# Attention and two MoE layers on one core: the first head pair's q and k transposed on TensorE instead of by DMA

## The chip, the cores and the metric

The kernel runs on one NeuronCore of a Trainium2 chip. Five engines work side by side, each through its own queue of instructions in order: TensorE (PE in the profile, its weight loads PEld), VectorE (DVE), ScalarE (ACT), GpSimd (POOL) and SyncE (SP), which here issues nearly all DMAs. The metric is the device time of one execution in microseconds, the median of several runs; lower is better.

## What is computed

Attention with a top-32 mask per row over 4 x 8 heads of 576 rows and 64 columns, a feed-forward layer with softplus on the 2304 tokens, and a layer of 8 experts of which each token uses one:

```
scores = scale * q @ k^T                    # 4 batches, 8 heads, 576 x 576
kth    = 32nd largest of each row
scores = where(scores >= kth, scores, -1e9)
attn   = softmax(scores);  x = attn @ v     # heads side by side: 2304 x 512
g      = softplus(x @ w_in) @ w_out         # 512 -> 2048 -> 512
e      = argmax(g @ w_gate)                 # one of 8 experts for each token
out    = gate * (relu(g @ w1[e]) @ w2[e])   # 512 -> 1024 -> 512
```

All inputs are float32. The scores and the first product of the feed-forward layer are made of fp16 parts: a number is split into its fp16 value and the fp16 of what that leaves.

## The kernel before

*Stages.* `part_one` does attention and the feed-forward layer, `part_two` the experts. In `part_one` two heads of one batch make a pair: q, k and v of a pair are loaded as tiles of 128 partitions (64 for each head) of 9 rows times 64 columns. There are 72 groups of scores on the normal path; a group holds two blocks of 128 queries, and a pair feeds two groups in the first sweep. `w_in` and `w_out` are loaded in 32 blocks and decoded (`decode`, L247 to L253) while attention is under way, and feed-forward work (`layer1` L596, `layer2` L636) runs between the groups once its tokens are there.

*Preparing a pair.* `prep_load` (L326) loads q, k, v into single buffers, so that the next pair's load waits for the last reader of this one's. `prep_split` (from L353) writes for k and then for q the fp16 value (ScalarE, L367) and the rest (L368, VectorE for the first pair, GpSimd for all others) side by side into a tile `st` (for the first two q: `p16`, printed as p). A DMA transposition turns k into `kt` (L370); two turn q, one for each head, into `q1` (L373). Two plain DMAs copy q1 into `q2` with the halves of the partitions swapped (L374, L375). v is split (L380, L381) and goes by six small DMAs into `v16` (L385 to L387). `magnitudes` (L335) sums absolute values for a later test; its outputs but for the sums are scrap. For the first pair it reads into scrap behind the split, for the others into the q2 that comes.

*A group.* `emit_scores` multiplies q1 and q2 by kt into two tiles of PSUM, `sa` (columns 0 to 255) and `sb` (256 to 575) (L406), and ScalarE copies sa to SBUF (L416). `emit_softmax` selects on VectorE: L446 to L451 make a tournament out of sa and sb, L456 to L472 take out the 32 largest in four rounds of eight. ScalarE copies sb (L452), which frees it for the next group, and L480 to L492 build the masked exponentials p on ScalarE and GpSimd, which a DMA transposition turns (L494) for the product with v (L509).

*What sets the order.* The kernel is written in the order of its steps, each with a priority; a scheduler with a model of the engines' times puts all instructions of the program in one order for each engine. The two preparations' tiles of PSUM, `sb` and `h` (of `ps_s`, one buffer, and `ps_h`, two), stand unused at the start. A last sweep without a fast path (`flags` is None, run again only where a test fails) isn't executed here.

The lines in question are few. Before, in `prep_split`:

```
if i == 0:
    nc.sync.dma_start_transpose(out=kt, in_=st...)                 # L370
else:
    for h in range(2):
        nc.sync.dma_start_transpose(out=q1[:, h], in_=st[64 * h:64 * h + 64]...)   # L373
nc.sync.dma_start(q2[0:64], q1[64:128])                            # L374
nc.sync.dma_start(q2[64:128], q1[0:64])                            # L375
```

Of the kernel before, what the change touches and what calls it, by code (L numbers as in the profile page):

```python
# [8 lines left out]
F32 = mybir.dt.float32  # L9
F32R = mybir.dt.float32r  # L10
F16 = mybir.dt.float16
I32 = mybir.dt.int32
U32 = mybir.dt.uint32
AF = mybir.ActivationFunctionType
# [5 lines left out]
B, H, S, D = 4, 8, 576, 64  # L20
NT, DM, DFF = 2304, 512, 2048
E, F2 = 8, 1024
R = 9
# [71 lines left out]
def attn_moe_moe2(ctx, tc, q, k, v, w_in, w_out, w_gate, w1, w2, out):  # L95
    nc = tc.nc
    const = ctx.enter_context(tc.tile_pool(name="const", bufs=1))
    dram = ctx.enter_context(tc.tile_pool(name="dram", bufs=1, space=DRAM))
    nc.scalar.preload_act_table_set("natural_log_exp_and_others")
    ident = const.tile([128, 128], F32, name="ident")  # L100
    make_identity(nc, ident)


    before = const.tile([128, 128], F32, name="before")
    ones = const.tile([128, 128], F32, name="ones")
# [3 lines left out]
    iota_e = const.tile([128, E], F32, name="iota_e")  # L109
# [3 lines left out]
    reg_e = const.tile([128, E], F32, name="reg_e")  # L113
# [3 lines left out]
    wg = const.tile([128, KD, E], F32, name="wg")  # L117
# [7 lines left out]
    def clear_table():  # L125
        with tc.tile_pool(name="fill", bufs=1) as p:
            fill = p.tile([128, (E * NT + SLOT) // 128], I32, name="fill")
            nc.gpsimd.iota(fill, pattern=[[0, (E * NT + SLOT) // 128]], base=TRASH, channel_multiplier=0)
            nc.sync.dma_start(table.rearrange("(p a) o -> p (a o)", p=128), fill)
# [5 lines left out]
    ids = const.tile([128, 4 * B + 2], I32, name="ids")  # L135
    for i in range(2):
        h = ids[64 * i:64 * i + 64]
# [3 lines left out]
    flags = const.tile([128, B * NP * R], F32, name="flags")  # L141
# [35 lines left out]
    def run(halves):  # L177
        nc.vector.memset(done, 0.0)
        clear_table()
        with ExitStack() as p:  # L180
            late = part_one(tc, p, q, k, v, w_in, w_out, const, ident, before, ones, iota_e, reg_e, wg, ids,
                            ohcum, done, early, table, rows, flags if halves else None, sums, w_sums, e_sums, kths)
        args = w1, w2, out, ident, ones, ohcum, done, early, late, table, rows, meta, left, rare
        with ExitStack() as p:
            part_two(tc, p, *args, (check, again) if halves else None, True)

        rv = nc.values_load(rare[0:1, 0:1], min_val=0, max_val=256)
        with tc.If(rv > 0):
            with ExitStack() as p:
                part_two(tc, p, *args, None, False)  # L190
            if halves:

                fv = nc.values_load(again[0:1, 0:1], min_val=0, max_val=128)
                with tc.If(fv > 0):
                    nc.vector.memset(ohcum, 0.0)
                    run(False)

    run(True)


def part_one(tc, ctx, q, k, v, w_in, w_out, const, ident, before, ones, iota_e, reg_e, wg, ids,
             ohcum, done, early, table, rows, flags, sums, w_sums, e_sums, kths):
    nc = tc.nc
    late = []

    def pool(name, bufs, **kw):
        return ctx.enter_context(tc.tile_pool(name=name, bufs=bufs, **kw))
# [13 lines left out]
    ps_s = pool("ps_s", 1, space=PSUM)  # L221
    ps_m = pool("ps_m", 1, space=PSUM)
    ps_h = pool("ps_h", 2, space=PSUM)
# [108 lines left out]
    def magnitudes(m, junk):  # L332
        src, bd = pair[m]
        for i, t in enumerate(src):
            nc.scalar.activation(junk, t, AF.Abs, accum_out=bd[:, i:i + 1])  # L335

    def prep_scale(m):
# [12 lines left out]
            nc.scalar.activation(src[i], src[i], AF.Copy, scale=sc[:, i:i + 1])  # L350
        pair[m] = (*src, sc)

    def prep_split(m):  # L353
        qn, kn, vn, sc = pair[m] if flags is None else (*pair[m][0], None)
        sub = nc.vector if m < DVS else nc.gpsimd
        q1 = kv.tile([128, 2, R, D], F16, name="q1")
        q2 = kv.tile([128, 2, R, D], F16, name="q2")
        kt = kv.tile([128, R, 128], F16, name="kt")
        if flags is not None and m >= LATEJ:
            magnitudes(m, q2[:, 0].rearrange("p r d -> p (r d)"))  # L360
        for i, xs in enumerate((kn, qn)):
            xv = xs.rearrange("p (r d) -> p r d", d=D)
            if i and m < ST0:
                st = row.tile([128, R, 2, D], F16, name="p16", bufs=PB if flags is not None else 2)
            else:
                st = stg.tile([128, R, 2, D], F16, name="st")
            nc.scalar.activation(st[:, :, 0, :], xv, AF.Copy)  # L367
            sub.tensor_tensor(out=st[:, :, 1, :], in0=xv, in1=st[:, :, 0, :], op=ALU.subtract)  # L368
            if i == 0:
                nc.sync.dma_start_transpose(out=kt, in_=st.rearrange("p r s d -> p (r s d)"))  # L370
            else:
                for h in range(2):
                    nc.sync.dma_start_transpose(out=q1[:, h], in_=st[64 * h:64 * h + 64].rearrange("p r s d -> p (r s d)"))  # L373
        nc.sync.dma_start(q2[0:64], q1[64:128])  # L374
        nc.sync.dma_start(q2[64:128], q1[0:64])  # L375

        v16 = kv.tile([128, 2, 5, 2 * D + 2], F16, name="v16")
        vs = stg.tile([128, R, 2 * D + 2], F16, name="vs")
        xv = vn.rearrange("p (r d) -> p r d", d=D)
        nc.scalar.activation(vs[:, :, 0:D], xv, AF.Copy)  # L380
        sub.tensor_tensor(out=vs[:, :, D + 2:], in0=xv, in1=vs[:, :, 0:D], op=ALU.subtract)  # L381
        nc.gpsimd.memset(vs[:, :, D:D + 2], 1.0)
        for h in range(2):
            src = vs[64 * h:64 * h + 64]
            nc.sync.dma_start(v16[0:64, h], src[:, 0:R:2])  # L385
            nc.sync.dma_start(v16[64:128, h, 0:4], src[:, 1:R:2])
            nc.sync.dma_start(v16[64:128, h, 4], src[:, 8])  # L387
        if flags is not None and m < LATEJ:
            magnitudes(m, row.tile([128, R, 2, D], F16, name="p16", bufs=PB if flags is not None else 2).rearrange("p r s d -> p (r s d)")[:, :R * D])
        pair[m] = (q1, q2, kt, v16, sc)  # L390
# [378 lines left out]
    for b, hp, ts in visits:  # L769
# [3 lines left out]
        m = len(pairs) - 1 - pairs[::-1].index((b, hp))  # L773
# [4 lines left out]
    for i, gr in enumerate(groups):  # L778
        for m, kd in gr:
            b = pairs[m][0]  # L780
# [11 lines left out]
    for i in range(-1, n + LAG):  # L792
# [5 lines left out]
        while done_prep < len(pairs) and when[done_prep] <= i:  # L798
            with tc.high_priority(offset=A_PREP):
                if to_scale:  # L800
                    prep_scale(to_scale.pop()[0])
                prep_split(done_prep)
                if done_prep + RB < len(pairs):
                    prep_load(done_prep + RB)
                if done_prep + 1 < len(pairs):
                    to_scale.append((done_prep + 1, i + SCALE))
            done_prep += 1
# [298 lines left out]
```

## Time and profile before

| | |
|---|---|
| median of 3 runs | 1065.49 us (1062.65 to 1066.71) |
| the profiled execution, its own time | 1060.82 us |
| its span, from the first to the last instruction | 1059.1 us |
| busy in the span: PE, DVE, ACT, POOL | 889.8, 853.0, 801.3, 603.0 us |
| mean granted clock of TensorE | 0.935 |

The profile shows one execution. Busy shares over the whole span mix stages that have different limits, so the rows below are taken by stretch and, for the first 60 us, by instruction. A wait is shown in brackets behind the instruction that waited: the idle time of its engine ahead of it and what ended it.

### The profile page before, as it was taken

Reading aid. Unit: us, or ns where it says so; the run is one execution under the profiler, and the core shown is the slowest. Engines: PE = TensorE matmul, PEld = TensorE weight load, DVE = VectorE, ACT = ScalarE, POOL = GpSimd, SP = SyncE. Lnnn points to the kernel's source line nnn. Section 1 sums busy time; section 2 is a strip of 40 time slices with the busy share of each in tenths; the row PEclk is TensorE's granted clock in tenths of the full one; section 3 lists DMA queues with packets and bytes.
Section 4 is the critical chain, followed back from the end, with each engine's and each line's share of the span. In section 5 each row is a group of like instructions: output and inputs, shape, how many; then the busy total and the mean of one; then the engine's idle time right before and its main releaser. Section 6 shows DMA issues by size and latency. Waiting matters only on the chain.

```text
span 1059.1 us, 22197 instructions
## 1 busy us (share of the span) xinstructions
PE 889.8 (84%) x7146; PEld 659.0 (62%) x7146; DVE 853.0 (81%) x3021; ACT 801.3 (76%) x1866; POOL 603.0 (57%) x631
## 2 busy tenths in 40 slices
PE   1124379666989797998999999999999999999994
PEld 0012256344656565665666667666787999999993
DVE  5789999899988688997889999965357987777774
ACT  5889899888799678897998898863677655555553
POOL 3889898998678587776877877762001022111111
PEclk9986579777999989998999999999999999999998
DMA  7897898985889987659876755564301667766760
GB/s 189 202 216 165 201 202 176 200 173 100 129 117 171 124 131 136 108 85 150 156 155 113 116 85 98 80 93 124 112 11 32 164 214 240 246 221 220 234 213 24
DMA packets 295859, 156.97 MB, mean 148 GB/s; under 512 B 257524, under 2 KB 257652, under 8 KB 295732
## 3 DMA queue, kind: packets, MB, share of 16 engines
q1 hardware_dynamic: 292116, 145.73, 65.2%
q0 software_dynamic: 3616, 9.72, 2.6%
q8 instruction: 58, 0.95, 0.4%
q14 instruction: 69, 0.57, 0.2%
HBM read 77.89 MB, written 11.11 MB: 84 GB/s over the span
## 4 chain that ended last, share of the span: by engine, by line
PE 47%; DVE 13%; DMA 9%; ACT 8%; POOL 6%; issue 4%; SPq 1%; POOLq 0%; ACTq 0%; DVEq 0%
PE h L937 10%; PE y L950 9%; PE h L596 9%; PE y L636 8%; DVE mx L472 3%; PE y L633 3%; DVE wk L468 3%; POOL e L481 2%; DMA vn<-in_v_dram 2%; DMA kt<-st 2%; DMA pT<-p 2%; PE m L509 1%; PE sb L406 1%; POOL p L492 1%; ACT e L482 1%
## 5 line engine op out<-in xcount | busy, mean ns | idle before, releaser
L636 PE MATMUL y<-w_out_s,g 128*128 128x512 f32 x480 | 233.7, 610 | 5.3 <-ACT g L611 4.7
L596 PE MATMUL h<-xT,w_in_s 128*128 128x256 f16 (+1 forms) x1920 | 224.5, 267 | 9.1 <-POOL w_in_s L260 3.2
L596 PEld LDWEIGHTS <-w_in_s 128*128 128x128 f16 x1920 | 173.6, 100 | 70.2 <-issue 43.6
L481 POOL TENSOR_TENSOR e<-s,e 128x576 f32<-128x576 f32 x144 | 202.5, 1421 | 16.9 <-ACT e L480 16.5
L472 DVE MAX8 mx<-wk 128x8 f32<-128x128 f32 (+2 forms) x432 | 200.8, 500 | 0.1
L492 POOL TENSOR_TENSOR p<-e,p 128x512 f16<-128x512 f32 x144 | 167.3, 1162 | 0.0
L406 PEld LDWEIGHTS <-q 128*128 128x128 f16 (+1 forms) x640 | 56.1, 109 | 175.5 <-issue 127.6
L468 DVE MATCH_REPLACE8 wk<-mx,wk 128x128 f32<-128x128 f32 (+1 forms) x432 | 144.6, 341 | 0.1
L636 PEld LDWEIGHTS y<-w_out_s,g 128*128 128x128 f32 x480 | 83.7, 195 | 69.0 <-issue 57.6
L917 POOL DMA_INDIRECT out_dram<-ot,idx x19 | 19.5, 1028 | 175.7 <-DVE ot L916 172.9
L482 ACT ACTIVATE e<-e,bias 128x576 f32<-128x576 f32 x144 | 110.5, 768 | 11.0 <-POOL e L481 10.4
L406 PE MATMUL sa<-kt,q 128*128 128x256 f16 (+1 forms) x320 | 53.0, 305 | 77.0 <-DMA kt<-st 22.9
L937 PEld LDWEIGHTS h<-xT,wf 128*128 128x128 f32 x864 | 111.8, 191 | 5.3 <-ACT wf L898 0.2
L937 PE MATMUL h<-xT,wf 128*128 128x256 f32 x864 | 113.9, 283 | 0.0
L950 PE MATMUL y<-wf,hT 128*128 128x512 f32 x432 | 112.8, 398 | 0.0
L406 PE MATMUL sb<-kt,q 128*128 128x320 f16 (+1 forms) x320 | 63.1, 340 | 50.9 <-ACT s L452 50.8
L480 ACT ACTIVATE e<-s,kths 128x576 f32<-128x576 f32 x144 | 105.0, 766 | 0.9
L509 PEld LDWEIGHTS <-pT 128*128 128x128 f16 (+1 forms) x1440 | 88.2, 107 | 24.4 <-issue 18.3
L509 PE MATMUL m<-v,pT 128*128 128x65 f16 (+1 forms) x1440 | 95.2, 202 | 9.5 <-DVE x L536 4.9
L490 ACT ACTIVATE p<-e 128x576 f16<-128x576 f32 x144 | 97.4, 678 | 5.0 <-DMA pT<-p 4.3
L491 POOL TENSOR_TENSOR p<-e,p 128x64 f16<-128x64 f32 x144 | 46.1, 320 | 73.6 <-ACT p L490 72.2
L610 ACT ACTIVATE sa<-h 128x256 f32<-128x256 f32 (+1 forms) x160 | 56.3, 352 | 40.1 <-PE h L596 39.3
(213 smaller groups left out, 1817.1 us busy)
## 6 DMA issues: line engine op xcount, KB each, us to landing
w1r<-in_moe_w_dram SPq DMA_DIRECT2D x20, 1024.0 KB
w2r<-in_moe_w_dram SPq DMA_DIRECT2D x20, 1024.0 KB, 6.6
w<-in_moe_w_in_dram SPq DMA_DIRECT2D x16, 512.0 KB, 4.2
w<-in_moe_w_out_dram SPq DMA_DIRECT2D x16, 512.0 KB
rows<-xr SPq DMA_DIRECT2D x37, 128.2 KB, 2.7
qn<-in_q_dram SPq DMA_DIRECT2D x16, 288.0 KB, 3.6
kn<-in_k_dram SPq DMA_DIRECT2D x16, 288.0 KB, 3.1
vn<-in_v_dram SPq DMA_DIRECT2D x16, 288.0 KB, 4.7
```

Source lines behind the costliest of these rows:

```text
L406: last_qk[0] = nc.tensor.matmul(ps[p0:p1], lhsT=qs[:, h, r0:r1, :].rearrange("p r d -> p (r d)"), rhs=kt[:, k0:k1, cs], start=first, stop= ...
L468: nc.vector.match_replace(out=to, in_to_replace=mx[:, i, 8 * j:8 * j + 8], in_values=src[i], imm_value=NEG)
L472: nc.vector.max(out=mx[:, i, 8 * j + 8:8 * j + 16], in_=src[i])
L480: nc.scalar.activation(e[i], s[i], AF.Relu, bias=kths[:, 2 * gi + i], scale=-K_UP)
L481: nc.gpsimd.tensor_tensor(out=e[i], in0=s[i], in1=e[i], op=ALU.subtract)
L482: nc.scalar.activation(e[i], e[i], AF.Exp, bias=bt[:, i], scale=SCORE)
L492: nc.gpsimd.tensor_tensor(out=p16[:, S + D:], in0=e[i][:, 0:S - D], in1=p16[:, 0:S - D], op=ALU.subtract)
L509: nc.tensor.matmul(o[:, h, 0:D + 1], lhsT=pT(r), rhs=v16[:, h, c, 0:D + 1], start=r == 0, stop=r == R - 1)
L596: nc.tensor.matmul(hps[:, :n], lhsT=w_in_s[:, c, j, p, o:o + 128], rhs=xT[:, 0:len(u.tiles), r, c, :], start=m == 0, stop=m == 3 * KD - 1)
L636: nc.tensor.matmul(u.y[i], lhsT=g[:, cs], rhs=w_out_s[:, f, :], start=f == 0, stop=f == KF - 1)
L937: nc.tensor.matmul(h, lhsT=w1f[:, a, c, :], rhs=xT[:, b, c, :], start=n == 0, stop=n == 3 * KD - 1)
L950: nc.tensor.matmul(y[i], lhsT=hT[g][:, a, i * 128:i * 128 + 128], rhs=w2f[:, b, :], start=g == 0 and n == 0, stop=g == KF2 - 1 and n == 2)
```

## The change

A second identity in fp16 is made on VectorE. For the first pair alone, a new function `turned` transposes the nine blocks of 128 columns by products with that identity, for q into `sb` and for k into two `h` tiles of PSUM. q1 is copied out of PSUM by VectorE in one instruction, kt by ScalarE (eight blocks) and VectorE (the ninth). The copies of q1 into q2 and all other pairs stay as they are. k is still split ahead of q in the code.

```diff
@@ -99,6 +99,8 @@
     nc.scalar.preload_act_table_set("natural_log_exp_and_others")
     ident = const.tile([128, 128], F32, name="ident")
     make_identity(nc, ident)
+    ident16 = const.tile([128, 128], F16, name="ident16")
+    nc.vector.tensor_copy(ident16, ident)
 
 
     before = const.tile([128, 128], F32, name="before")
@@ -178,7 +180,7 @@
         nc.vector.memset(done, 0.0)
         clear_table()
         with ExitStack() as p:
-            late = part_one(tc, p, q, k, v, w_in, w_out, const, ident, before, ones, iota_e, reg_e, wg, ids,
+            late = part_one(tc, p, q, k, v, w_in, w_out, const, (ident, ident16), before, ones, iota_e, reg_e, wg, ids,
                             ohcum, done, early, table, rows, flags if halves else None, sums, w_sums, e_sums, kths)
         args = w1, w2, out, ident, ones, ohcum, done, early, late, table, rows, meta, left, rare
         with ExitStack() as p:
@@ -202,6 +204,7 @@
              ohcum, done, early, table, rows, flags, sums, w_sums, e_sums, kths):
     nc = tc.nc
     late = []
+    ident, ident16 = ident
 
     def pool(name, bufs, **kw):
         return ctx.enter_context(tc.tile_pool(name=name, bufs=bufs, **kw))
@@ -350,6 +353,22 @@
             nc.scalar.activation(src[i], src[i], AF.Copy, scale=sc[:, i:i + 1])
         pair[m] = (*src, sc)
 
+    def turned(st, to, i):
+        if i:
+            ps = ps_s.tile([128, 2, 512], F32, name="sb").rearrange("p a b -> p (a b)").bitcast(F16)
+            parts = [(ps[:, 128 * r:128 * r + 128], r) for r in range(R)]
+        else:
+            ps = [ps_h.tile([128, 512], F32, name="h").bitcast(F16) for _ in range(2)]
+            parts = [(ps[r // 8][:, 128 * (r % 8):128 * (r % 8) + 128], r) for r in range(R)]
+        for t, r in parts:
+            nc.tensor.transpose(t, st[:, r].rearrange("p s d -> p (s d)"), ident16)
+        if i:
+            nc.vector.tensor_copy(to.rearrange("p h r d -> p r h d"),
+                                  ps[:, :R * 128].rearrange("p (r h d) -> p r h d", h=2, d=D))
+        else:
+            nc.scalar.activation(to[:, 0:8], ps[0].rearrange("p (r c) -> p r c", c=128), AF.Copy)
+            nc.vector.tensor_copy(to[:, 8], ps[1][:, :128])
+
     def prep_split(m):
         qn, kn, vn, sc = pair[m] if flags is None else (*pair[m][0], None)
         sub = nc.vector if m < DVS else nc.gpsimd
@@ -366,7 +385,9 @@
                 st = stg.tile([128, R, 2, D], F16, name="st")
             nc.scalar.activation(st[:, :, 0, :], xv, AF.Copy)
             sub.tensor_tensor(out=st[:, :, 1, :], in0=xv, in1=st[:, :, 0, :], op=ALU.subtract)
-            if i == 0:
+            if m == 0 and flags is not None:
+                turned(st, kt if i == 0 else q1, i)
+            elif i == 0:
                 nc.sync.dma_start_transpose(out=kt, in_=st.rearrange("p r s d -> p (r s d)"))
             else:
                 for h in range(2):
```

The scheduler orders the new program anew; line numbers behind the new code are 21 higher in `prep_split` and 3 higher ahead of it.

SP, from the second pair's first load on, before (q_170 and q_171 are q1 and q2 of the first pair, q_205 is q1 of the second):

```order
L326 DMA qn<-in_q_dram 128x576
L373 DMA_TRANSPOSE q_170<-p_177 128x9x64
L370 DMA_TRANSPOSE kt<-st 128x9x128
L373 DMA_TRANSPOSE q_170<-p_177 128x9x64
L385 DMA v_184<-vs 64x5x130
L374 DMA q_171<-q_170 64x1152
L375 DMA q_171<-q_170 64x1152
L373 DMA_TRANSPOSE q_205<-p_215 128x9x64 x2
```

and after (q_172 and q_173 are q1 and q2 of the first pair, L394 and L391 the second pair's transpositions):

```order
L329 DMA qn<-in_q_dram 128x576
L329 DMA kn<-in_k_dram 128x576
L395 DMA q_173<-q_172 64x1152
L396 DMA q_173<-q_172 64x1152
L406 DMA v_207<-vs 64x5x130
L407 DMA v_207<-vs 64x4x130
L408 DMA v_207<-vs 64x130
L329 DMA vn<-in_v_dram 128x576
L241 DMA w<-in_moe_w_in_dram 128x1024
L394 DMA_TRANSPOSE q_228<-p_238 128x9x64
L391 DMA_TRANSPOSE kt<-st 128x9x128
L394 DMA_TRANSPOSE q_228<-p_238 128x9x64
```

The first pair's three transpositions are gone, the copies into q2 stand ahead of the v16 DMAs and the second pair's k load directly behind its q load.

ScalarE, from the first decode step to the first copies of scores, before (L247 and L251 are decode steps, L258 and L259 the steps of w_in_s, L335 and L367 a magnitude and a split of the second pair):

```order
L247 ACTIVATE y<-w 128x512
L251 ACTIVATE w<-w 128x512
L247 ACTIVATE y<-w 128x512
L251 ACTIVATE w<-w 128x512
L367 ACTIVATE p_215<-qn 128x9x64
L258 ACTIVATE w_in_s,w_sums<-t 128x512
L259 ACTIVATE w_in_s<-t 128x512
L335 ACTIVATE q_206,sums<-qn 128x576
L258 ACTIVATE w_in_s,w_sums<-t 128x512
L259 ACTIVATE w_in_s<-t 128x512
L416 ACTIVATE s<-sa 128x2x256 x2
```

and after (L250 and L254, L261 and L262, L338 and L386 are the same steps, L369 is kt of the first pair, L437 the copy of scores):

```order
L250 ACTIVATE y<-w 128x512
L254 ACTIVATE w<-w 128x512
L369 ACTIVATE kt<-h 128x1024
L250 ACTIVATE y<-w 128x512
L254 ACTIVATE w<-w 128x512
L338 ACTIVATE q_229,sums<-qn 128x576
L386 ACTIVATE p_238<-qn 128x9x64
L386 ACTIVATE st<-kn 128x9x64
L261 ACTIVATE w_in_s,w_sums<-t 128x512
L262 ACTIVATE w_in_s<-t 128x512
L338 ACTIVATE q_229,sums<-kn 128x576
L437 ACTIVATE s<-sa 128x2x256
```

The copy into kt stands behind the first decode step, and ahead of the first copy of scores now stand the second pair's k split and k magnitude; the second block's steps of w_in_s have moved behind it.

## Rows read from the trace of the kernel before

**Rows 1.** The page's first line: the span

```profile
span 1059.1 us, 22197 instructions
```

**Rows 2.** Busy time by stretch; PEclk is the granted clock

```profile
core 0: us, PE busy (x) PEld busy (x) DVE busy (x) ACT busy (x) POOL busy (x), PEclk, DMA share, GB/s
...
48.00:60.00 12.00, 0.66 (x2) 0.13 (x2) 9.06 (x30) 10.27 (x21) 12.00 (x14) 1.00 0.88 215
60.00:84.00 24.00, 9.36 (x108) 7.01 (x109) 19.21 (x66) 19.31 (x39) 21.14 (x24) 0.74 1.00 216
84.00:120.00 36.00, 14.25 (x155) 9.48 (x154) 35.93 (x129) 32.36 (x64) 32.63 (x32) 0.59 0.73 166
...
300.00:400.00 100.00, 91.15 (x732) 60.34 (x731) 79.23 (x326) 80.12 (x197) 71.44 (x74) 0.93 0.90 140
...
600.00:700.00 100.00, 97.98 (x877) 66.45 (x876) 98.06 (x407) 88.22 (x209) 73.84 (x78) 1.00 0.53 86
```

**Rows 3.** The same view, two stretches of the start

```profile
8.00:10.00 2.00, 0.00 (x0) 0.00 (x0) 0.20 (x1) 0.85 (x2) 0.00 (x0) 1.00 1.46 312
18.00:20.00 2.00, 1.40 (x6) 0.62 (x5) 1.43 (x4) 0.90 (x2) 1.15 (x1) 1.00 0.38 71
```

**Rows 4.** VectorE in order of time, four of its waits: start, us, instruction, idle before

```profile
18.50 0.43 DVE L446 TENSOR_TENSOR sb<-sb,s 128x256 f32<-128x256 f32 x1 [5.95 <-PE sb L406]
...
30.10 0.70 DVE L249 TENSOR_SCALAR y<-y 128x512 uint32<-128x512 uint32 x1 [2.03 <-ACT y L247]
...
50.58 0.43 DVE L446 TENSOR_TENSOR sb<-sb,s 128x256 f32<-128x256 f32 x1 [2.26 <-ACT s L416]
...
82.56 0.43 DVE L446 TENSOR_TENSOR sb<-sb,s 128x256 f32<-128x256 f32 x1 [0.68 <-PE sb L406]
```

**Rows 5.** The start in order of time, all engines

```profile
4.34 0.76 DVE L368 TENSOR_TENSOR p<-qn,p 128x576 f16<-128x576 f32 x1 [2.44 <-ACT p L367]
...
6.92 1.33 SPq L373 DMA_TRANSPOSE q<-p  x1
...
8.36 1.85 SPq L370 DMA_TRANSPOSE kt<-st  x1
...
9.15 0.62 ACT L247 ACTIVATE y<-w 128x512 f32<-128x512 f32 x1 [1.70 <-DMA w<-in_moe_w_in_dram]
...
12.87 0.37 PE L406 MATMUL sa<-kt,q 128*128 128x256 f16 x1 [12.87 <-DMA kt<-st]
...
13.56 0.49 SPq L374 DMA_DIRECT2D q<-q  x1
...
16.80 0.80 PE L406 MATMUL sa<-kt,q 128*128 128x256 f16 x3 [3.30 <-DMA q<-q]
...
17.76 0.57 ACT L416 ACTIVATE s<-sa 128x512 f32<-128x512 f32 x1
...
21.37 0.42 SPq L326 DMA_DIRECT2D kn<-in_k_dram  x1
```

**Rows 6.** Groups by line: busy us, mean ns of one, idle before

```profile
L450 DVE COPY wk<-sb 128x128 f32<-128x128 f32 x72 | 20.1, 280 | 0.0
L451 DVE TENSOR_TENSOR wk<-sb,s 128x512 f32<-128x512 f32 x72 | 48.9, 679 | 0.0
L416 ACT ACTIVATE s<-sa 128x512 f32<-128x512 f32 x72 | 42.0, 583 | 3.4 <-PE sa L406 1.6 <-POOL e L481 1.6
L452 ACT ACTIVATE s<-sb 128x640 f32<-128x640 f32 x72 | 49.8, 692 | 5.6 <-DVE wk L451 4.5 <-DVE m L674 0.8
```

**Rows 7.** SP's queue, first 60 us, waits: us, times, longest

```profile
SPq L373 <- DMA table<-fill: 1.4, 1, 1.4
```

**Rows 8.** GpSimd in order of time: its first L481

```profile
32.27 2.79 POOL L481 TENSOR_TENSOR e<-s,e 128x576 f32<-128x576 f32 x2 [3.60 <-ACT e L480]
```

**Rows 9.** The chain that ended last, in order of time, two pieces

```profile
735.32 1.72 PE y L636 x4
...
738.35 1.72 PE y L636 x4
```

## The prediction

> **What bounds the kernel now.** I read the busy time by stretch first, then the start by instruction. Over its span of 1059.1 us [rows 1] the kernel fills one engine after the other: GpSimd works 12.00 of 12 us from 48 us on, the DMA engines stand at a share of 1.00 from 60 to 84 us, VectorE works 35.93 of 36 us from 84 on, TensorE 97.98 of 100 us from 600 on [rows 2]. Ahead of these full stages lies a start in which nothing is full: from 8 to 10 us VectorE works 0.20 of 2 us, from 18 to 20 us the DMA engines are at 0.38 [rows 3]. What the start wastes, full stages cannot make up, and the change touches the start alone.
>
> In the start the reader should follow one wait. VectorE sits idle for 5.95 us, until 18.50 us, for the first scores [rows 4]. The scores need kt (the turned k) and q1, q2 (the turned q, and a copy of it with the two heads swapped). The transposition into kt is issued at 8.36 us and its first reader starts at 12.87; the copies into q2 are issued from 13.56 on and their first reader starts at 16.80 [rows 5].
>
> **The change, part by part.** *Removed:* three DMA transpositions, of which the first occupies SP's queue from 6.92 for 1.33 us and the second from 8.36 for 1.85 [rows 5]; the third lies between them and the copies into q2. Everything that SP issues stands behind them, the second pair's k among it, which goes out at 21.37 only [rows 5]. The three read 2 x 128 x 1152 x 2 bytes = 0.59 MB. At the 216 GB/s that the DMA engines move while they are full [rows 2] this is worth 2.7 us of all of them.
>
> The Trainium skill says (Advanced Engine Details and Errata, "X-Bar Transpose (TRN2)") that such transpositions are as fast as plain DMAs, with 350 to 400 GB/s to be expected, which speaks against the change: by that it frees 1.5 to 1.7 us of DMA and not 2.7. No row here shows such a rate.
>
> *Added on TensorE:* 18 products with the identity, of 128 columns. Three score products of 256 columns took 0.80 us in the same place [rows 5], 0.27 us each, so one of 128 costs between half of that, 0.13, and the whole: nine cost 1.2 to 2.4 us. I take 1.2, since the columns are halved. TensorE has nothing else to do before 12 us, so only the chain pays for it.
>
> *Added on VectorE:* a cast of the identity, in idle time, and the copy of 1152 columns from PSUM into q1. L450 copies 128 columns in 280 ns, L451 does 512 in 679 [rows 6]: 1.04 ns a column, so 280 + 1024 x 1.04 = 1345 ns; I take 1.4 us. *Added on ScalarE:* 1024 columns of kt. L416 copies 512 in 583 ns, L452 640 in 692 [rows 6]: 0.85 ns a column, so 692 + 384 x 0.85 = 1.02 us.
>
> *The chain of q.* VectorE ends the split of q at 4.34 + 0.76 = 5.10 [rows 5]; the nine products end at 6.3. The copy into q1 waits, as the first transposition did, for the landing of table<-fill, for which SP sat until 6.92 [rows 5, 7]. It runs from 6.9 to 8.3, and the copies into q2 go out at 8.3 instead of 13.56. With the same 3.2 us to their reader, q2 is there at 11.6 instead of 16.8. *The chain of k.* Its products end near 7.6, but ScalarE's copy stands behind the first decode step of w_in in the new order, L247 and L251, whose load landed at 9.15 and which take some 0.62 each [rows 5]. So kt is there at 10.4 + 1.0 = 11.4 instead of 12.87. TensorE gives the first scores near 12.5 instead of 17.6: 5 us earlier.
>
> *Where these 5 us go.* Not to VectorE's first selection. In the new order ScalarE has eight instructions of 512 or 576 columns between kt and the first copy of scores (two decode steps, two magnitudes, two splits, two steps of w_in_s). At 0.58 to 0.69 us each [rows 6] they take 4.6 to 5.5 us, with the read-outs of three accumulators a little more, so I place the copy at 17.2, against 17.76 [rows 5]. VectorE starts half a microsecond earlier and no more. What is won is work done early. When GpSimd comes to the first L481, the new order has put three more instructions of such a size ahead of it (one decode addition, one subtraction for w_in_s, one split), some 3.7 us by L481's own 1.40 [rows 8]; and I place that L481 near 29.5 instead of 32.27, at the end of VectorE's selection for the first group.
>
> *What reaches the full stages.* VectorE has ten idle spells from 30.10 to 82.56 us, 10.3 us in all (the first, the longest and the last stand in [rows 4]). I carried the new order on by hand, with the durations of before, up to the fourth group of scores: VectorE starts it near 47.2 instead of 50.58 [rows 4], with one decode less done (two steps, 1.4 us), so 2.0 us ahead. Of the five spells behind that, 5.1 us of waits for scores and decodes, I take half, since GpSimd is full there but itself some us ahead. Sum 2.0 + 2.5 = 4.5, less 0.5 for the added copies where they meet a busy engine: **4 us**. The DMA engines allow it: 2.7 us are taken off them, and the loads of the second pair, which now go out ahead, fill what lies open before 20 us. The ends are 0 (ScalarE's order eats all) and 10.3 (no idle spell left). Behind 84 us I count the gain as kept.
>
> The profiled execution took 1060.82 us, 1.7 over its span; the median of the runs is 1065.49. The 4 us come off that median: 1061.5.
>
> **The rivals.** *Absorbed.* The first scores come early and nobody picks them up: ScalarE's order holds VectorE, and DMA engines that are full from 60 to 84 us [rows 2] set when the later pairs come. Against it: in the new order of SP the second pair's k goes out straight behind its q, in the first 7 us, not at 21.37. Time: 1065.5.
>
> *No idle spell left.* The second and third pairs come so early that VectorE never waits before 84 us: 10.3 us, 1055. Against it: the raw tiles of q, k and v are single, so that each load waits for the pair before it.
>
> The Trainium skill gives (VectorE: DVE Perf Modes, "The three transpose paths") 390 ns for a 128x128 block on TensorE and 1309 ns for the DMA crossbar, and advises TensorE where PSUM will do; for 18 blocks that makes 16.5 us, an estimate that ends at 1049. The trace doesn't bear it out: from the issue of kt's nine blocks to their reader it was 4.5 us, 0.5 us a block [rows 5], and the results must go back to SBUF besides. I give it no more than a share of this rival.
>
> *Slower by re-sequencing.* The scheduler orders the whole program anew. From the 23rd to the 45th group of scores, ScalarE's new order has one to four feed-forward steps less behind it than before at the same group, mostly two (17 against 19 at the 24th, counted by L610). A step of TensorE is 738.35 - 735.32 = 3.03 us [rows 9], two are 6 us. If TensorE's idle time there, 8.85 of 100 us from 300 on [rows 2], doesn't take them back, they are left for the stage where TensorE is full, and the time is 1071.5. It decides at the point from which TensorE stays full. For it: any order of DMAs other than the old can put a late load in front of a queue. Against it: at the last group both orders have 115 steps behind them.
>
> *Not what it says* would mean that the products wait for something that is later than the DMA was. In the order they stand first on TensorE, behind VectorE's splits alone; I leave it out.
>
> **How the numbers follow.** Forecast (2 to 6 us won): 0.46. Absorbed: 0.23. All of the idle spells, or more: 0.16. Slower: 0.15. What a measurement of this kernel can tell from no change is about 0.5%, 5.3 us: faster is below 1060.2, slower above 1070.8. Faster takes the 0.16 and somewhat under half of the forecast: 0.36. Slower takes 0.13, since the re-sequencing need not cost all of the 6 us. Same: 0.51. The range goes from 1053, a little past the end of all idle spells, to 1070, most of the two steps; what lies outside is the far part of either rival.
>
> **What would show it.** Right: products from about 5.2 us on, copies into q2 issued near 8.3, first scores near 12.5 and yet VectorE's first L446 near 18; its fourth group near 47; its idle time from 18 to 84 us down by some 4 us. Wrong: a copy from PSUM of over 2 us; kt later than 12.9; a fourth group not before 50; or a VectorE that is 4 us ahead at 84 us and not at 700, which would be the re-sequencing.

## The result, and the profile after

The changed kernel takes 1075.14 us (median of 11 runs, 1069.40 to 1083.42), the kernel before 1065.93 (11 runs beside them, 1061.62 to 1070.29). The ratio is 1.0091, 95% interval 1.0063 to 1.0120: 9 us slower, where 4 us faster were forecast. It lies outside the range (1053 to 1070), on the other side. The profiled execution took 1073.94 us; its page begins with

```profile
span 1072.1 us, 22248 instructions
```

13.0 us more than [rows 1]. The start of the changed kernel, in order of time, all engines (start, us, engine, line, operation, idle time before and its releaser; lines behind the new function stand 21 further down than in the kernel before):

```profile
5.24 1.14 PE L364 MATMUL sb<-ident,p 128*128 128x128 f16 x9 [5.24 <-DVE p L387]
...
7.06 0.76 DVE L366 COPY q<-sb 128x1152 f16<-128x1152 f16 x1 [0.64 <-DMA table<-fill]
...
7.84 0.54 SPq L395 DMA_DIRECT2D q<-q  x1
...
10.84 1.01 ACT L369 ACTIVATE kt<-h 128x1024 f16<-128x1024 f16 x1
...
11.91 0.37 PE L427 MATMUL sa<-kt,q 128*128 128x256 f16 x1 [4.29 <-ACT kt L369]
...
14.89 0.80 PE L427 MATMUL sa<-kt,q 128*128 128x256 f16 x3 [2.34 <-DMA q<-q]
...
17.26 0.43 DVE L467 TENSOR_TENSOR sb<-sb,s 128x256 f32<-128x256 f32 x1 [3.26 <-ACT s L437]
...
28.98 2.76 POOL L502 TENSOR_TENSOR e<-s,e 128x576 f32<-128x576 f32 x2
...
43.24 0.41 DVE L467 TENSOR_TENSOR sb<-sb,s 128x256 f32<-128x256 f32 x1
...
101.56 0.41 DVE L467 TENSOR_TENSOR sb<-sb,s 128x256 f32<-128x256 f32 x1
```

Up to the fourth group the change does what it should: the last but one row is that group's first instruction, at 43.24 us instead of 50.58 [rows 4]. The last row is the ninth group, at 101.56 us; in the kernel before it starts at 99.8. The lead is gone by then. The stretches of [rows 2], in the changed kernel:

```profile
core 0: us, PE busy (x) PEld busy (x) DVE busy (x) ACT busy (x) POOL busy (x), PEclk, DMA share, GB/s
48.00:60.00 12.00, 3.76 (x36) 2.71 (x36) 6.76 (x19) 8.71 (x18) 9.35 (x10) 1.00 0.85 194
60.00:84.00 24.00, 6.98 (x72) 5.22 (x72) 19.94 (x68) 16.31 (x31) 18.62 (x20) 0.75 0.93 208
84.00:120.00 36.00, 14.19 (x150) 9.71 (x150) 34.55 (x121) 31.87 (x64) 31.97 (x32) 0.59 0.64 149
300.00:400.00 100.00, 88.56 (x785) 59.43 (x783) 79.73 (x333) 83.99 (x210) 74.63 (x79) 0.97 0.91 144
600.00:700.00 100.00, 95.21 (x854) 64.49 (x854) 96.40 (x389) 89.11 (x209) 74.71 (x80) 1.00 0.54 84
```

The work that was pulled forward leaves gaps behind it: GpSimd works 9.35 of 12 us from 48 us on, where it was full, and VectorE 34.55 instead of 35.93 of 36 us from 84 on. Between its fourth group and 84 us VectorE now waits 8.9 us, where it waited 5.1 before; 5.6 of them are for decode steps, and these wait for the loads of w_out, for example:

```profile
56.07 0.62 ACT L250 ACTIVATE y<-w 128x512 f32<-128x512 f32 x1 [3.20 <-DMA w<-in_moe_w_out_dram]
56.72 0.70 DVE L252 TENSOR_SCALAR y<-y 128x512 uint32<-128x512 uint32 x1 [2.62 <-ACT y L250]
```

That takes the lead away, but the 13 us are not lost there. TensorE, which is the bound in the later stages, shows where they are. The same view of three stretches, first of the kernel before, then of the changed one:

```profile
270.00:725.00 455.00, 430.32 (x3858) 292.37 (x3857) 393.06 (x1638) 379.57 (x930) 332.78 (x356) 0.97 0.74 119
556.00:606.00 50.00, 49.55 (x449) 34.40 (x448) 47.95 (x200) 44.23 (x106) 40.71 (x46) 1.00 0.73 116
700.00:725.00 25.00, 25.00 (x258) 17.88 (x255) 10.97 (x59) 12.94 (x34) 13.84 (x17) 1.00 0.62 91
```

```profile
270.00:725.00 455.00, 418.17 (x3728) 281.04 (x3727) 385.62 (x1602) 373.76 (x917) 328.16 (x351) 0.97 0.75 118
556.00:606.00 50.00, 42.25 (x375) 29.44 (x374) 41.12 (x175) 37.14 (x88) 35.38 (x40) 0.97 0.70 103
700.00:725.00 25.00, 21.36 (x174) 14.12 (x174) 7.94 (x31) 10.63 (x28) 11.73 (x15) 0.86 0.71 89
```

From 270 to 725 us TensorE works 12.15 us less, 10.94 of them in two places (7.30 from 556 to 606, 3.64 from 700 to 725), 540 us behind the edit. The attention isn't late there: the last group of scores still starts 1.2 us earlier than before (692.72 against 693.94 us). The feed-forward steps are: 3.5 us ahead at the 86th, near 560 us, some 8 behind near 700, 11.8 from 730 on. What stands in the two places? All engines of the changed kernel in order of time, around the second place:

```profile
707.02 1.16 POOL L578 TENSOR_TENSOR xh<-x,xh 128x512 f16<-128x512 f32 x1
707.02 2.78 SPq L515 DMA_TRANSPOSE pT<-p  x2
708.33 0.98 POOL L726 DMA_INDIRECT table<-ids,dsti  x1 [0.16 <-issue]
709.90 1.49 SPq L579 DMA_TRANSPOSE xT<-xh  x1
...
717.24 0.63 ACT L577 ACTIVATE xh<-xtail 128x512 f16<-128x512 f32 x1 [5.70 <-DMA xT<-xh]
...
718.58 2.72 PE L617 MATMUL h<-xT,w_in_s 128*128 128x256 f16 x12 [3.64 <-ACT sa L631]
```

L726 writes the numbers of 128 tokens to their places in the routing table in DRAM, by an indirect DMA of GpSimd; there is one such write for each of the 18 token tiles. The transposition xT, issued 1.6 us behind one, is not there before 717 us. ScalarE waits for it, since xh has a single buffer, and TensorE waits for ScalarE. The rows of the first place are of the same kind: a table write at 557.61 and the six copies of v16 issued from 557.18 to 560.52 us.

```profile
566.87 0.68 ACT L401 ACTIVATE vs<-vn 128x576 f16<-128x576 f32 x1 [6.38 <-DMA v<-vs]
...
570.12 0.43 DVE L467 TENSOR_TENSOR sb<-sb,s 128x256 f32<-128x256 f32 x1 [5.65 <-ACT s L437]
...
570.13 0.87 PE L427 MATMUL sa<-kt,q 128*128 128x256 f16 x4 [4.99 <-ACT s L437]
```

A third write, at 589.84, meets two transpositions into pT, and ScalarE waits 2.75 us for them, until 598.23. From issue to landing a write itself takes this long (the line's own summary in the changed kernel, for the six of its 18 writes whose landing is in the trace whole):

```profile
DMA to landing us min/median/max: 6.8/8.1/10.7
```

### The profile page after: what moved, and what is told of

It is laid out like the page before. It is cut to its first block, busy times and chain, and to the rows that moved or that the text cites. A ratio compares the mean times of both kernels' runs of the same rounds, so it can differ in the third digit from the quotient of the medians.

```text
span 1072.1 us, 22248 instructions
## 1 busy us (share of the span) xinstructions
PE 892.6 (83%) x7164; PEld 658.0 (61%) x7164; DVE 851.6 (79%) x3024; ACT 800.9 (75%) x1867; POOL 603.3 (56%) x631
## 4 chain that ended last, share of the span: by engine, by line
PE 37%; DVE 16%; DMA 16%; ACT 11%; POOL 9%; issue 5%; SPq 4%; POOLq 0%; ACTq 0%; DVEq 0%
PE h L958 10%; PE y L971 9%; PE h L617 6%; DVE mx L493 5%; PE y L657 4%; DMA pT<-p 4%; DVE wk L489 4%; POOL e L502 3%; PE y L654 3%; DMA w<-in_moe_w_in_dram 3%; DMA v<-vs 2%; POOL p L513 2%; DMA q<-st 2%; ACT p L511 1%; ACT e L501 1%
## 5 line engine op out<-in xcount | busy, mean ns | idle before, releaser
L617 PE MATMUL h<-xT,w_in_s 128*128 128x256 f16 (+1 forms) x1920 | 229.2, 269 | 16.9 <-ACT sa L631 11.4
L530 PEld LDWEIGHTS <-pT 128*128 128x128 f16 (+1 forms) x1440 | 87.9, 107 | 21.9 <-issue 19.1
L971 PEld LDWEIGHTS y<-wf,hT 128*128 128x128 f32 x432 | 76.7, 189 | 14.5 <-DVE ohcum L718 1.5
```

What stands on the lines that cost most here:

```text
L530: nc.tensor.matmul(o[:, h, 0:D + 1], lhsT=pT(r), rhs=v16[:, h, c, 0:D + 1], start=r == 0, stop=r == R - 1)
L617: nc.tensor.matmul(hps[:, :n], lhsT=w_in_s[:, c, j, p, o:o + 128], rhs=xT[:, 0:len(u.tiles), r, c, :], start=m == 0, stop=m == 3 * KD - 1)
L971: nc.tensor.matmul(y[i], lhsT=hT[g][:, a, i * 128:i * 128 + 128], rhs=w2f[:, b, :], start=g == 0 and n == 0, stop=g == KF2 - 1 and n == 2)
```

## The experiments

**Theory** after this reading: the scheduler's new order costs the time, not the products. After the first four runs it was put more closely: the order decides which transfers fall into the 8 us behind a table write, called a hole below. **Rivals:** the products and the early start cost lasting time in any order; or the waits belong to the order and would come without the writes.

*How an order is held.* A table in the kernel gives, for each engine, the order of the instructions that both kernels have (the other kernel's, or its own with something moved). Once the program is traced, one edge from each instruction to the next is added, which sets the order of issue and waits for nothing. Instructions that only one kernel has find their own place (shortened at the dots):

```
+        for s in step:
+            k += s
+            if last is not None:
+                tc.add_manual_dep(mine[k], last.name, ... NoSync ..., reason="order")
+            last = mine[k]
```

**1. Orders exchanged.** The first two kernels differ in the table alone from the changed kernel and the kernel before.

> The changed kernel, with every instruction that both kernels have held in the order that the kernel before has on its engine; only the 18 products, the cast and the three copies find their own places. Theory (the scheduler's new order costs the time): the 9 us go away, 1060 to 1066 us, and the stalls of 556 to 606 us and 707 to 725 us are not there. Rival (the products and their start cost lasting time, whatever the order): it stays at 1072 to 1078. Third (order and products share it): about 1070.

> The kernel before, DMA transpositions and all, with every instruction that both have held in the order of the changed kernel. Theory (the order costs the time): 1073 to 1080 us, slower than before without a single product with the identity, with the same stalls near 560 to 606 and 707 to 725 us. Rival (the products cost it): 1064 to 1067, as before.

> The changed kernel in its own order up to the 54th group of scores (some 540 us), and in the order of before from there on. Theory (the loss lies in the order behind 550 us, at the three stalls): 1057 to 1066 us, as the attention was up to 9.9 us ahead at 550 us. Rival (the loss is already set by what the order did ahead of 550 us, where feed-forward steps fell up to 14 us behind): 1072 to 1078.

> The mirror: the changed kernel in the order of before up to the 54th group of scores and in its own order behind. Theory (loss in the order behind 550 us): 1070 to 1078 us, with the stalls at 556 to 606 and 707 to 725 us. Rival (loss set ahead of 550 us): 1060 to 1067.

Measured: e1 1.0056 of before (1.0027 to 1.0084), e2 1.0182 (1.0144 to 1.0219), e3 1.0000 (0.9975 to 1.0025), e4 1.0177 (1.0136 to 1.0218). e2 holds not one product with the identity and is slower than the changed kernel: an order alone can cost some 18 us (1086.57 us beside 1069.27). e3 has the whole start of the changed kernel and costs nothing, so that the products cost little lasting time, if any. Where e3 differs from the changed kernel's order lies behind the 54th group of scores, and that takes the 9 us away; e4 puts the changed kernel's order behind that group on the first half of the order before, and loses some 18 us. e2 and e4 thus lost more than their ranges had, and e3, at 1068.25 us, lies 2 us above its own. But e1 missed in kind: with the old order everywhere 1060 to 1066 us were expected, and it took 1075.07 beside 1069.27. Its groups of scores stand within 1.1 us of those of the kernel before up to 306 us (the first one at 18.6: held in the old order, the early products win nothing), then it loses time at single waits for kt, pT and xT. "The order" is thus too coarse a name for the cause. What e1 and the changed kernel share was seen when TensorE's idle time was split by the table writes (table below).

**2. The table writes taken out, and moved.** In the first two kernels a small copy on GpSimd stands in the place of each write (shortened at the dots):

```
-        wr = nc.gpsimd.indirect_dma_start(out=table, ...)
+        if flags is not None:
+            nc.gpsimd.tensor_copy(dsti, dsti)
+            return
+        wr = nc.gpsimd.indirect_dma_start(out=table, ...)
```

> The changed kernel in its own order, but the indirect writes of the routing table (L726) are left out of part one; a GpSimd copy of 128x1 stands at the place of each, so the table keeps its fill and part two gathers the zero row. In the profile of the changed kernel no transfer that is issued with or just after such a write lands before it, 8 us later, and TensorE stands idle for 16.6 us in the 12 us behind those of 270 to 725 us, against 5.6 in the kernel before (20.3 and 19.1 elsewhere). Theory (the 9 us are made by what falls into these holes): 1055 to 1064 us, 11 to 20 less than the changed kernel, and within 4 us of the next run. Rival (the waits belong to the new order and come anyway): 8 to 10 us above the next run.

> The kernel before in its own order, with the same writes (L705) left out of part one in the same way. Theory: it wins 3 to 8 us only, 1057 to 1063, since its holes cost TensorE 5.6 us. Rival (the writes cost both kernels the same): it wins as much as the changed kernel does, and the distance of 9 us between the two stays.

Measured: 0.9724 (0.9690 to 0.9759; 1038.73 us beside 1067.62) and 0.9723 (0.9694 to 0.9753; 1038.21). The two kernels take the same time, 29 us below the kernel before. The 9 us between them are gone, as the theory has it; but the writes cost the kernel before some 29 us too, where 3 to 8 were expected from the 5.6 us of idle time behind them. Part two writes less here (no row finds its token), yet the gain is nearly all part one's: from its first product to its last part two takes 213.78 us in e6 as in the kernel before, and 217.04 in e5 against 215.40 in the changed kernel; only what follows is 1.2 to 1.5 us shorter. TensorE from 270 to 725 us, e5 and then e6:

```profile
270.00:725.00 455.00, 445.60 (x4003) 301.92 (x4000) 406.58 (x1740) 388.40 (x962) 325.04 (x359) 1.00 0.70 129
```

```profile
270.00:725.00 455.00, 440.45 (x3983) 300.02 (x3981) 404.40 (x1740) 387.71 (x955) 325.93 (x360) 1.00 0.69 127
```

15 and 10 us more than the kernel before has there, and at a mean granted clock of 1.00 instead of 0.97. Without the writes the new order is, by this row, the fuller one.

In the next two, all writes are there, and some stand at other places of GpSimd's order; nothing else moves.

> The changed kernel with three of its 18 table writes put later in GpSimd's order and nothing else moved: the 8th by six instructions (from 557.6 to about 569 us, behind the landing of v16), the 9th by four (589.8 to about 595.5), the 12th by two (708.3 to about 712.7, so that xT, issued at 709.9, can land). Theory: 1063 to 1069 us, since the three stalls of 556 to 606 and 707 to 725 us shrink by half or more. Rival (the stalls are the order's own, the write only happens to be near): 1072 to 1078 as the changed kernel.

> The kernel before with one table write put later and nothing else moved: the 12th by three instructions of GpSimd, from 704.2 to about 709.1 us, so that xT, issued at 709.17, falls into its hole as in the changed kernel. Theory: 3 to 7 us slower than before, with TensorE idle near 715 to 720 and its granted clock down behind that. Rival (the place of the write is of no account): the time of before, within 1.5 us.

Measured: e7 1.0002 (0.9974 to 1.0031), e8 1.0071 (1.0040 to 1.0103). Three instructions of GpSimd, each put two to six places later, take away the whole loss of the changed kernel; one instruction put three places later gives the kernel before most of it. A write was put later in both, with a gain in one and a loss in the other, so that it isn't the later place as such. In e7 the write comes at 710.41, xT had been issued at 707.57, and ScalarE's wait falls from 5.70 to 1.77 us:

```profile
710.90 0.63 ACT L577 ACTIVATE xh<-xtail 128x512 f16<-128x512 f32 x1 [1.77 <-DMA xT<-xh]
```

In e8 the write and xT meet as intended, and the rows of the changed kernel at 707 to 719 us come up in the kernel before (all engines, in order of time):

```profile
715.65 1.23 SPq L558 DMA_TRANSPOSE xT<-xh  x1
715.78 0.98 POOL L705 DMA_INDIRECT table<-ids,dsti  x1 [0.15 <-issue]
...
725.70 0.63 ACT L556 ACTIVATE xh<-xtail 128x512 f16<-128x512 f32 x1 [8.45 <-DMA xT<-xh]
...
726.75 2.78 PE L596 MATMUL h<-xT,w_in_s 128*128 128x256 f16 x24 [3.55 <-ACT sa L610]
```

**3. The writes put together.** If two writes that follow each other share one hole, fewer places cost less. In GpSimd's order table the first write of each pair is taken out and put directly in front of the second.

> The changed kernel in its own order, all 18 table writes kept, but each odd one of the first twelve put directly in front of the next in GpSimd's order (1 with 2, 3 with 4, to 11 with 12): 12 places instead of 18. All writes left out gave 29 us. Theory A (writes that follow each other share one hole): a third to a half of that is won where the stalls are, 1054 to 1064 us. Theory B (the holes add up, 16 us for two): 1066 to 1080, since a hole of 16 us outlasts every buffer.

> The kernel before in its own order with the same six pairs. Theory A: 1052 to 1061 us. Theory B: 1066 to 1080. By the runs without any write, in which both kernels took the same time, it stands within 4 us of the changed kernel in pairs under either.

> The same with the first twelve in three groups of four (9 places instead of 18). Theory A (one hole for a group): 1048 to 1062 us. Theory B (the holes add up, 32 us for four): 1080 us and more.

> The kernel before in its own order with the three groups of four. Theory A: 1047 to 1060 us. Theory B: 1080 us and more.

Measured in pairs: old order 0.9920 (0.9891 to 0.9950), new order 1.0052 (1.0033 to 1.0071). By the times alone e11 (1052.75 us) lies in theory A's range and e9 (1067.10) in theory B's, and the kernel before ran at 1060.07 beside them. The landings decide for A: of the pair issued at 548.88 and 550.17 us in e11 both have landed by 557.7, ahead of the next transposition at 559.3, and the twelve pairs of the two kernels take 8.7 to 12.2 us from the first issue to the last landing, as far as their landings are in the traces. But the two orders are 14 us apart where 4 were expected; why is open. The "fours" weren't fours: the kernel declares the writes independent of each other, which drops the edges between neighbours, and so only the first of each four moved, to the fourth. Measured as they ran, with 15 places instead of 18: new 1.0097 (1.0066 to 1.0127), old 1.0001 (0.9978 to 1.0025), no gain in either.

Left open was whether the new order has a cost of its own. For real groups each write of a group got its edges to the instructions ahead of and behind the group, and dsti eight buffers:

```
-        dsti = sm.tile([128, 1], I32, name="dsti")
+        dsti = sm.tile([128, 1], I32, name="dsti", bufs=8)
```

> In the runs meant as fours only the first write of each four had moved (to the fourth), the second and third stood at their own places; here all four stand together, so that the first twelve writes have three places (dsti gets 8 buffers for it). The changed kernel in its own order. If TensorE's loss is what falls into the holes behind writes, three holes cost less than six or nine: 0.985 to 0.998 of before. If the new order is slow by itself, 1.003 to 1.010 as in pairs.

> The kernel before in its own order with three groups of four. Holes: 0.983 to 0.993 of before, within 0.007 of the changed kernel in fours, since both took the same time without any write.

> The changed kernel with the first twelve writes at two places, six each. Holes: 0.980 to 0.995 of before, if six writes share one hole of 9 to 14 us; order by itself: 1.003 to 1.010; a hole that grows by 8 us with each write: 1.01 and more.

> The kernel before in its own order with two groups of six. Holes: 0.978 to 0.993 of before, within 0.007 of the changed kernel in sixes.

Measured in fours: new 1.0048 (1.0026 to 1.0071), old 0.9944 (0.9924 to 0.9964), 0.0104 apart: both missed, the new one at the number that stood for "order by itself". In sixes: new 0.9870 (0.9841 to 0.9899), old 0.9917 (0.9893 to 0.9940): now the new order is ahead. Six writes in e14 (GpSimd):

```profile
436.64 1.14 POOL L726 DMA_INDIRECT table<-ids,dsti  x1 [0.18 <-issue]
438.08 0.98 POOL L726 DMA_INDIRECT table<-ids,dsti  x1 [0.30 <-issue]
...
443.18 0.97 POOL L726 DMA_INDIRECT table<-ids,dsti  x1 [0.31 <-issue]
```

A transposition issued at 445.62 lands at 452.28 us, 9.1 us behind the issue of the last of the six. A larger group has a longer hole, though: from the first issue to the last landing the three fours of e13 take 18.0, 21.3 and 18.0 us and the two sixes of e14 15.5 and 20.1, twice a single write's 8 and far from four or six times it. By that, three fours hold the transfers up about as long as six pairs, two sixes for much less; this is read from the landings and not tried by itself. The new order is 1.0% behind the other in fours and 0.5% ahead in sixes; so it isn't slow by itself. e14, the changed kernel with twelve writes at two places, is by its ratio the fastest here that computes all of the reference, ahead of both kernels: 1053.57 us beside 1067.40.

**All runs side by side.** TensorE in the profiled execution, 270 to 725 us: its idle time, counted from its instructions and split into the 12 us behind a table write and the rest, and the time at the lower level of its granted clock (1.2 GHz), from the trace's record of the clock. The idle times add up to 455 less the busy time in the rows above (before: 5.6 + 19.1 = 24.7).

| kernel | idle behind a write | elsewhere | at the lower clock | ratio to before |
|---|---|---|---|---|
| before | 5.6 | 19.1 | 27.3 | 1 |
| changed | 16.6 | 20.3 | 23.9 | 1.0091 |
| e1 new, old order | 11.8 | 23.8 | 27.3 | 1.0056 |
| e2 old, new order | 18.4 | 18.8 | 27.3 | 1.0182 |
| e3 new order to group 54, then old | 5.3 | 19.2 | 17.1 | 1.0000 |
| e4 old order to group 54, then new | 15.3 | 25.9 | 30.7 | 1.0177 |
| e5, e6 no writes in part one (new, old) | 0, 0 | 9.4, 14.6 | 0, 3.4 | 0.9724, 0.9723 |
| e7 new, three writes moved | 5.3 | 18.1 | 17.1 | 1.0002 |
| e8 old, one write moved | 11.6 | 23.2 | 23.9 | 1.0071 |
| e9, e11 pairs (new, old) | 17.8, 4.6 | 10.7, 20.7 | 23.9, 6.8 | 1.0052, 0.9920 |
| e10, e12 first of four moved (new, old) | 14.3, 4.7 | 17.2, 24.0 | 27.3, 17.1 | 1.0097, 1.0001 |
| e13, e15 fours (new, old) | 17.2, 8.6 | 13.3, 19.6 | 27.3, 20.5 | 1.0048, 0.9944 |
| e14, e16 sixes (new, old) | 10.4, 6.3 | 11.2, 15.8 | 6.8, 20.5 | 0.9870, 0.9917 |

From the kernel before to the changed one the first column grows by 11.0 us, the second by 1.2, and the third doesn't grow. The idle time is not the whole price of the writes, however. e11 is as idle as the kernel before and 0.8% faster; what differs is the time at the lower clock, 6.8 us instead of 27.3. The same goes for the 29 us of e6: 10 us less idle time and 24 us less at the lower clock. That the writes bring the clock down by the waits that they make is thus likely, but not shown: no run changes the one without the other. Each value is one execution, and a kernel's runs spread over 10 us and more, so a single line is rough. e2 and e4 lose 5.1 and 4.1 us more between 725 and 745 us.

One part of the loss belongs to neither writes nor order. In the changed kernel and all nine runs built from it TensorE waits in part two at a place where the kernel before and the seven runs built from that don't (changed kernel, then before):

```profile
843.97 4.38 PE L971 MATMUL y<-wf,hT 128*128 128x512 f32 x18 [1.44 <-DVE ohcum L718]
```

```profile
830.36 4.34 PE L950 MATMUL y<-wf,hT 128*128 128x512 f32 x18
```

From its first product to its last part two takes 215.40 to 217.26 us in the former, 213.78 to 215.19 in the latter, whichever order is held and with or without writes; why, no run shows. It is 1.6 of the profile's 13.0 us, and 2.9 of what e1 loses. That the rest of e1's 0.56% comes from holes is argued from the first column alone, as the second grows by 4.7 us too; e1 without the writes wasn't tried.

## Why the prediction was wrong, point by point

- *The products*, 1.2 us for nine: 1.14 (the row at 5.24 us above). *ScalarE's copy of kt*, 1.02 us: 1.01; kt there at 11.4: the scores start at 11.91. *Copies into q2* issued at 8.3: 7.84. *First L446 near 18* although the scores are early: 17.26, held by ScalarE as described. *First L481 near 29.5*: 28.98. (The 3.7 us taken there for three instructions is not three times L481's 1.40, which makes 4.2.)
- *VectorE's copy from PSUM*, 1.4 us, was mis-sized: 0.76 us for 1152 columns, 0.66 ns a column. The rows it was taken from [rows 6] are float32 at 1.04 ns; this copy is float16. The Trainium skill (VectorE: DVE Perf Modes, "Why PSUM operands drop a tier") allows an operand from PSUM twice the plain rate at most, and float32 only the plain one; this row agrees.
- *The same 3.2 us to the reader of q2* was mis-sized: 7.05 us, from 7.84 to 14.89. In the new order the copies of v16 go out right behind, and the DMA engines move 374 GB/s from 8 to 10 us, against 312 before [rows 3]. The prediction read this start as one "in which nothing is full"; its own row has the DMA share at 1.46 there.
- *Fourth group near 47.2*: 43.24. The gain in the start was larger than forecast, 7.3 us instead of 3.4.
- *"Of the five spells behind that, 5.1 us of waits for scores and decodes, I take half"*: this step of the sum failed. Behind the fourth group VectorE's waits up to 84 us grew to 8.9 us instead of shrinking to 2.6, since the decode steps waited for their loads. Its idle time from 18 to 84 us fell by 0.85 us (11.41 to 10.56) and not by 4.
- *"Behind 84 us I count the gain as kept"*: this step failed too. At the ninth group the changed kernel is 1.8 us behind. Later it is ahead once more, by 2.45 to 9.76 us from the 35th to the 56th group, and without the writes it is still 8.65 us ahead at the last (666.30 us in e5, 674.95 in e6). It is worth nothing even then: TensorE must do the feed-forward steps whenever the attention ends, and the last of them ends only 1.9 us earlier in e5 (796.18 against 798.11), which the longer part two takes back.
- *What stood in no term of the sum*: the transfers behind a table write. The new order that came with the change let three writes meet v16, pT and xT, which cost the 9 us: with these three writes moved they are gone (e7), and with one write moved to such a place the kernel before loses 0.7% (e8).
- *Rival "slower by re-sequencing"* (0.15) came true in its sign and its clause "any order of DMAs other than the old can put a late load in front of a queue", not in its mechanism and size. It forecast two feed-forward steps of lag, 6 us, 1071.5. The steps did lag, by up to 15 us (the 32nd, near 324 us), and were 4.5 ahead again at the 69th. The price came from what was late: not a load but the transfers behind an indirect write, which neither the order nor [rows 2] shows unless the landing times of single transfers are read.
- *Absorbed* (0.23) is what the runs show of the change where no write is in the way: 0.9724 against 0.9723. Its reason was right in part: VectorE is held, though not by ScalarE's order or the later pairs but by the loads of w_out (the rows at 56 us); whether full DMA engines make these late wasn't tried.

## What to carry to other kernels

Where a scheduler orders the whole program, an edit of a few instructions is a re-ordering of everything: hold the old order (or exchange the two) before a gain or a loss is put down to the edit. Ask of the trace which transfers land much later than their kind's median and what was issued at that moment; here one small indirect write decided over every transfer beside it, and its place was worth more than the edit. A lead won by an engine that isn't the bound later is a lead in its own work, not in the end time.

## What the runs showed of the hardware

An indirect write of 128 words by GpSimd takes 8.1 us to land (median, the row above). A transfer of SP that hasn't landed within some 3 us of the write's issue lands only behind it: beside the write at 557.61 us the copy of v16 issued at 557.18 landed at 559.49, and the five issued from 557.87 to 560.52, usually there in 2.2 us (median of v16's copies), landed from 565.69 to 566.77 (the last records that the trace has of each). The same holds for all 24 transfers beside a single write whose two landings are whole in the traces (before, changed, e7, e8, e10): 8 landed within 3.1 us of the issue, 16 behind the write, none between. Writes issued 1.3 us apart share much of this time: 8.7 to 12.2 us for two, 15.5 and 20.1 for six. Why it is so long no run here shows.

The Trainium skill (DMA: Bandwidth & Descriptors, "SWDGE vs HWDGE vs iDMA") says that a DMA engine has different queues for the two kinds of descriptor generation and takes turns between them, and gives for one such DMA a fixed 2.0 us ("Anatomy of one DMA — SWDGE (gpsimd) path"). From these two a reader would not expect other transfers to stand still for 8 us; the landings here show that they do.

TensorE's clock can add to such a wait. TensorE has no work for 3.64 us up to 718.58 us; the mean granted clock of the two stretches of 5 us around and behind is 0.71 and 0.61, between its lower level (1.2 GHz) and its full one (2.4 GHz):

```profile
715.00:720.00 5.00, 1.42 (x7) 0.99 (x7) 0.20 (x1) 2.20 (x6) 1.33 (x3) 0.71 0.76 67
720.00:725.00 5.00, 5.00 (x13) 2.50 (x11) 0.00 (x0) 0.89 (x3) 0.00 (x0) 0.61 0.56 56
```

The twelve products at 718.58 us take 2.72 us; twelve of the same kind in e8 (718.23 us, clock 1.00) take 1.48. In e8 the wait is about as long, 3.55 us (the row at 726.75), and the clock stayed at 1.00, so that a wait of this length doesn't always bring it down.
